# Five block-diagonal blocks, a first block in halves, and search steps spaced by GpSimd's adds, in an FFT convolution with a routed FFN

## The chip, the core and the metric

The kernel runs on one core of a Trainium2 chip. The metric is the device time of one execution in microseconds (us). The core's engines have queues of their own and work side by side: TensorE (PE) multiplies matrices, VectorE (DVE), ScalarE (ACT) and GpSimd (POOL) do the elementwise work, SyncE (SP) issues the transfers. Data lies in SBUF; matmul results go to PSUM, from which another engine must take them.

## The reference

`x` has 8 sequences of 6336 positions and 128 features, `h` one such filter, all in float32. The first part is a causal convolution of every feature by FFT; the second picks the 128 positions with the highest score in each sequence, and adds a gated feed-forward network there and nowhere else.

```python
L = 2 * S                                  # S = 6336
Xf = np.fft.rfft(x, n=L, axis=1)
Hf = np.fft.rfft(h, n=L, axis=0)
y = np.fft.irfft(Xf * Hf[None], n=L, axis=1)[:, :S, :]
...
scores = np.einsum('bsd,d->bs', y, w_gate)
out = y.copy()
for b in range(B):                         # B = 8
    top_idx = np.argpartition(-scores[b], capacity)[:capacity]    # 128
    xe = y[b, top_idx]
    ye = np.maximum(xe @ w1, 0.0) @ w2     # 128 -> 1024 -> 128
    g = 1.0 / (1.0 + np.exp(-scores[b, top_idx]))
    out[b, top_idx] = y[b, top_idx] + g[:, None] * ye
```

## The kernel before

**Tiling.** The transforms are matmuls with tables, with 6336 = 99 x 64. The data is cut into eight units: a pair of sequences (four of them) times a half of the features (two). Unit i has its frequency data in one of two halves of a large SBUF tile (`slots`), i % 2, so that one unit can be transformed while the one before is finished.

**Stages.** Stage A (`stage_a`, L170 to L197) is the transform of 99 points. Its input comes in blocks of 8 per unit: blocks 0 to 7 are the filter `h`, 8 to 15 are unit 0, and 16 + 8i onwards are unit i + 1. `load_x` (L138 to L149) issues a block's load on SP's queue; a paced load has a one-element memset by VectorE ahead of it (L148), which holds it back until VectorE is there. `fold` (L151 to L167) has VectorE make the difference and the sum of a block's two parts. `stage_a` then works in two half blocks (`q` = 0 and 1), each with a PSUM pair of its own: either 16 matmuls of 50 rows and 99 columns (a quartered block, L185), or, for the blocks named in `whole` at L173, 8 matmuls of 128 rows and 198 columns against the block-diagonal table `fa2` (L179). A copy to SBUF follows, by ScalarE (L197) or, where the half is named in `dve`, by VectorE (L194): at the start the second halves of blocks above 9.

Stage B (`stage_b`, L247 to L257) does the second transform in 13 chunks of 8 frequencies (L225), multiplies by the filter (VectorE, L234), and GpSimd adds the two products (L245). `stage_b_first` (L263 to L295) is the joint part, which does the same for the filter and unit 0 together (PE L275, ScalarE L278, VectorE L287, GpSimd L290). Stage C (`stage_c`, from L318) and stage D (`stage_d`, from L354) go back: PE L332 with ScalarE's copy L336, PE L362 with ScalarE's copy L383 and the store to `out`. While stage C runs, VectorE weighs the columns for the scores (L313).

**PSUM.** `psb` hands out three pairs of banks in turn, `psm` two single banks. A tile can be filled again once the one before in its place has been read.

**The route.** For every pair of sequences a generator (`route`) yields between its steps: the scores (L400, L413), a search for the 128th highest key with 6 + 5 digits (`search`, L434 to L463), the places of the chosen rows (L478 to L502), the gather by GpSimd (L525), and then the feed-forward network (`expert`). One search step is a comparison with 7 thresholds (L442), a count (L445), a matmul that sums over the partitions (L451) and three short operations (L454 to L460), all but the matmul on VectorE.

**Order.** Each engine works its queue strictly in order, and the order is written out by a planner with two clocks, `t["pe"]` and `t["dve"]`, which add up constants: 0.7 for a half block of stage A, 0.24 for a frequency of stage B, 0.47 for a column of stage C, 0.89 for a tap of stage D. At a route step's yield, `after_dve(us)` (L56) sets VectorE's clock to the later of both plus `us` plus an allowance, `calm`, and the step after it may be taken 0.3 past that. `aside` (L670s) takes the next step if PE's clock has got there; outside stage D it also asks that VectorE's clock be less than 1.0 past PE's. `aside` is called at most taps of stage D and behind each piece of the plan.

**The main program.** At the start come the loads of the tables and of blocks 0 to 3, 44 small matmuls and a fill of two wide ones (L701) that compute nothing of use, the folds, and 16 blocks of stage A; then the joint part over 13 chunks. Then each unit i runs 32 items, 16 of stage C and 16 of stage D, and a dict `plan` says at which items a half block of unit i + 1 (items 0 to 8) or two of its stage B chunks (items 14 to 28; in unit 6 items 11 to 24) are put between. Unit 7 has nothing to prepare.

Of the kernel before, what the change touches and what calls it, by code (L numbers as in the profile page):

```python
# [12 lines left out]
ALU = mybir.AluOpType  # L13
# [5 lines left out]
N1, N2 = 99, 64  # L19
NE = 50  # L20
NU = 8
# [14 lines left out]
def conv_moe(ctx, tc, x, h, wg_d, w1, w2, fa_d, wb_d, wc_d, at_d, wgl_d, tri_d, cst_d, tw_d, fb_d, *out):  # L36
    nc = tc.nc
    v, act, pool, pe, sp = nc.vector, nc.scalar, nc.gpsimd, nc.tensor, nc.sync
# [7 lines left out]
    t = {"pe": 0.0, "dve": 0.0}  # L46

    def on_pe(us):
        t["pe"] += us

    def on_dve(us):
        t["dve"] = max(t["dve"], t["pe"]) + us

    calm = [0.0]

    def after_dve(us):  # L56
        on_dve(us + calm[0])
        return t["dve"] + 0.3

    due = []  # L60
# [11 lines left out]
    def psb():  # L72
        return pb_.tile([128, 2, 512], F32, tag="b", name="pb")

    def psm():
        return pm_.tile([128, 512], F32, tag="m", name="m")
# [9 lines left out]
    fa = cp.tile([128, 2, N1], F32, name="fa")  # L86
# [17 lines left out]
    acc = cp.tile([128, 2, 2, 2, N1], F32, name="acc")  # L104
# [28 lines left out]
    raw, odd = {}, {}  # L133
    two = cp.tile([128, 2, 512], F32, name="two")

    def load_x(g, paced=False):
        if g >= 8 * (NU + 1):
            return  # L138
        i, n = g // 8 - 1, g % 8
        if i < 0:  # L140
            raw[g] = flat[:, (n + 4) * 1024:(n + 5) * 1024].rearrange("p (s d n) -> p s d n", s=2, d=8)
        elif 8 + RX <= g < 16:
            raw[g] = low(0, 1024, g - 8 - RX).rearrange("p (s d n) -> p s d n", s=2, d=8)
        else:
            raw[g] = tp.tile([128, 2, 8, N2], F32, tag="x", name="xr", bufs=RX)
        src = h if i < 0 else x[i]
        if paced:
            v.memset(raw[g][0:1, 0, 0, 0:1], 0.0)  # L148
        sp.dma_start(out=raw[g].rearrange("p s d n -> p s (d n)"), in_=src[:, n].rearrange("s p w -> p s w"))  # L149

    def fold(g, eng, part=0):  # L151
        if g >= 8 * (NU + 1):
            return
        a = raw[g]
        if g < 16:
            o = low(1, 512, g % 7)
        elif g % 8 % 3 < 2:
            o = two[:, g % 8 % 3]
        else:
            o = low((g // 8 - 1) % 2, 512, 6)  # L160
        odd[g] = o.rearrange("p (d n) -> p d n", d=8)
        o = odd[g]
        if part < 2:
            eng.tensor_tensor(out=o, in0=a[:, 1], in1=a[:, 0], op=ALU.subtract)
        if part != 1:
            eng.tensor_tensor(out=a[:, 0], in0=a[:, 0], in1=a[:, 1], op=ALU.add)  # L166
# [3 lines left out]
    def stage_a(g, r, dve=(), halves=(0, 1)):  # L170
        a, o = raw[g], odd[g]
        n = g % 8
        whole = g in (2, 4, 6, 8, 10, 12)  # L173
        for q in halves:
            pt = psb()
            for d in range(4):
                if whole:
                    for c in range(2):
                        pe.matmul(pt[c * 64:c * 64 + 64, d // 2, d % 2 * 2 * N1:(d % 2 + 1) * 2 * N1],  # L179
                                  (o if c else a[:, 0])[:, q * 4 + d], fa2[:, c], start=True, stop=True)  # L180
                    continue
                for b, c in ((0, 0), (1, 1), (0, 1), (1, 0)):
                    rows = slice(b * 64, b * 64 + NE)
                    src = (o if c else a[:, 0])[rows, q * 4 + d]
                    pe.matmul(pt[c * 64:c * 64 + 64, b, d * N1:(d + 1) * N1], src, fa[rows, c], start=True, stop=True)  # L185
            j = n % 4 * 4 + q * 2
            dst = ys[r].rearrange("p (g b j) k t -> p g b j t k", g=2, b=2)[:, n // 4, :, j:j + 2]
            on_pe(0.7)
            if whole:
                src = pt[:, :, 0:4 * N1].rearrange("p j (t b k) -> p b j t k", t=2, b=2)  # L190
            else:
                src = pt[:, :, 0:4 * N1].rearrange("p b (j t k) -> p b j t k", j=2, t=2)
            if q in dve:
                v.tensor_copy(out=dst, in_=src)  # L194
                on_dve(0.9)
            else:
                act.copy(out=dst, in_=src)  # L197
# [31 lines left out]
    def times(r, ci, banks, ht):  # L229
        k0, kn = kchunks[ci]  # L230
        yv = ys[r].rearrange("p (j c) k t -> p j c k t", c=2)[:, :, :, k0:k0 + kn]

        def mult(dst, c, t):
            v.tensor_tensor(out=dst, in0=banks[c][:, 0:kn * 64].rearrange("p (k b j t) -> p k b j t", k=kn, b=2, t=2),  # L234
                            in1=ht[t].rearrange("p k (j t) -> p k j t", t=2).unsqueeze(2).broadcast_to(
                                [128, kn, 2, 16, 2]), op=ALU.mult)

        for c in range(2):
            tx = tp.tile([128, KC, 64], F32, tag="t", name="tx", bufs=3)[:, 0:kn]
            dst = yv[:, :, c].rearrange("p (b j) k t -> p k b j t", b=2)  # L240
            mult(dst, 0, c)
            mult(tx.rearrange("p k (b j t) -> p k b j t", b=2, t=2), 1, 1 - c)
            on_dve(kn * 0.155)
            d3 = yv[:, :, c].rearrange("p j k t -> p k j t")
            pool.tensor_tensor(out=d3, in0=d3, in1=tx.rearrange("p k (j t) -> p k j t", t=2),  # L245
                               op=ALU.add if c else ALU.subtract)

    def stage_b(i, ci):
        r, u = i % 2, i % 2
        k0, kn = kchunks[ci]  # L250
        pair = psb()
        banks = [pair[:, 0], pair[:, 1]]
        over_k(r, wts.pop((r, ci)), ci, banks)
        ht = hts.pop((u, ci))
        times(r, ci, banks, [ht[:, 0, 0:kn], ht[:, 1, 0:kn]])
        load_w(r, ci + RW)
        later(t["dve"], lambda: load_h(u, ci + RH))  # L257

# [427 lines left out]
    with tc.manual_schedule():  # L686
# [3 lines left out]
        plain = acc.rearrange("p t b c k -> p (t b c k)")[:, 0:128]  # L690
        v.memset(plain, 1.0)
        pt = psb()
# [5 lines left out]
        def fill(n):  # L698
            pt = psm()
            for _ in range(n):  # L700
                pe.matmul(pt, plain, wide, start=True, stop=True)  # L701

        wide = acc.rearrange("p t b c k -> p (t b c k)")[:, 0:512]
        v.memset(wide[:, 128:512], 1.0)
        fill(2)
        pool.memset(fa2, 0.0)
        for o in (0, 1):
# [22 lines left out]
        for i in range(NU):  # L730
# [2 lines left out]
            g0 = 16 + 8 * i  # L733
            plan = {}
            if i < NU - 1:
                for n, at_item in enumerate((0, 0, 0, 2, 2, 2, 4, 4, 4, 6, 6, 6, 8, 8, 8, 8)):
                    plan.setdefault(at_item, []).append(("a", n))
                for n, at_item in enumerate((14, 16, 18, 20, 23, 26, 28) if i < NU - 2 else (11, 13, 16, 18, 20, 22, 24)):
                    plan[at_item] = [("b", k) for k in range(2 * n, min(NC, 2 * n + 2))]
            at_first = 9 if i < NU - 1 else 2  # L740
            calm[0] = 0.45 if i < NU - 1 else 0.0
            for item in range(32):
                place[0] = item
                strand = cs if item < 16 else ds
# [184 lines left out]
```

## Time and profile before

| | us |
|---|---|
| median of 3 runs | 874.43 (874.38 to 876.86) |
| the profiled execution | 875.82 |
| its span, first to last instruction | 874.0 |
| the start, up to the joint part's first full run of matmuls | 41.67 |
| the joint part and the first half blocks of unit 1, up to stage C's first full run | 50.40 (41.67 to 92.07) |
| TensorE's granted clock | 0.999 |

Most of the span's time is in stages C, D, A and B of the eight units. These are the profile's rows for the path that ended last, by line, and for the costliest groups (line, engine, operation, count; busy us, mean ns; idle us just before them and what ended most of it):

```profile
PE 76%; DVE 16%; DMA 3%; issue 3%; POOL 1%; ACT 1%; POOLq 0%; DVEq 0%; ACTq 0%; SPq 0%
...
L332 PE MATMUL pb<-wc,slots 64*99 64x128 f32 x4096 | 236.9, 271 | 1.8 <-POOL slots L290 0.9
L362 PE MATMUL pb<-slots,at 99*99 99x256 f32 (+1 forms) x1056 | 234.0, 374 | 0.6 <-ACT yt L383 0.5
```

A group's idle time counts only on the engine that the row names. The rows of stage C (L332) and stage D (L362) carry 470.9 us of TensorE's work between them and hardly wait.

### The profile page before, as it was taken

The numbers are of one execution on the slowest core, as the hardware profiler recorded it, in microseconds if no ns is written. First come the engines' busy times: TensorE is split into PE (matmuls) and PEld (weight loads), VectorE is DVE, ScalarE is ACT, GpSimd is POOL, SyncE is SP. The second block draws the span as 40 slices with busy tenths as digits, with TensorE's granted clock in tenths as the row PEclk, the third lists the DMA queues.
The fourth block names the chain that finished last, engine by engine and source line by source line (L and its number), as shares of the span: only waits on it lengthen the run. The fifth ranks groups of instructions, "written<-read, shape, count | busy, mean of one in ns | idle before, by whom it ended". The sixth has DMA issues, their size and how long they took to land.

```text
span 874.0 us, 36824 instructions
## 1 busy us (share of the span) xinstructions
PE 852.9 (98%) x16420; PEld 759.4 (87%) x16420; DVE 699.2 (80%) x1609; ACT 348.5 (40%) x407; POOL 323.6 (37%) x269
## 2 busy tenths in 40 slices
PE   9999999999999999999999999999999999999996
PEld 7899898889987998889987899789988899879875
DVE  6678966677599979888399979979379997987771
ACT  5533661157212751157301672137501373125422
POOL 0078106610455016630455105740256304567005
PEclk9999999999999999999999999999999999999999
DMA  8678568766595667666376576845558445752151
GB/s 288 226 251 323 193 194 265 238 191 214 159 286 178 206 189 248 211 196 202 112 227 220 172 226 187 272 152 192 185 152 275 142 156 161 231 164 78 37 184 32
DMA packets 76377, 170.73 MB, mean 195 GB/s; under 512 B 9785, under 2 KB 26135, under 8 KB 76218
## 3 DMA queue, kind: packets, MB, share of 16 engines
q1 hardware_dynamic: 75194, 167.32, 59.6%
q8 instruction: 129, 2.11, 1.0%
q0 software_dynamic: 1024, 1.05, 0.5%
q14 instruction: 30, 0.25, 0.1%
HBM read 135.38 MB, written 32.96 MB: 193 GB/s over the span
## 4 chain that ended last, share of the span: by engine, by line
PE 76%; DVE 16%; DMA 3%; issue 3%; POOL 1%; ACT 1%; POOLq 0%; DVEq 0%; ACTq 0%; SPq 0%
PE pb L332 26%; PE pb L362 18%; PE pb L185 11%; PE pb L225 11%; DVE tx L234 4%; DVE slots L234 4%; PE pb L275 4%; DMA ht<-hd 2%; DVE cmp L442 2%; PE pb L179 2%; PE m L606 1%; PE m L619 1%; PE m L400 1%; DVE num L445 1%; DVE thr L458 1%
## 5 line engine op out<-in xcount | busy, mean ns | idle before, releaser
L245 POOL TENSOR_TENSOR slots<-slots,tx 128x512 f32<-128x512 f32 (+1 forms) x182 | 233.4, 1314 | 427.6 <-DVE tx L234 411.6
L332 PE MATMUL pb<-wc,slots 64*99 64x128 f32 x4096 | 236.9, 271 | 1.8 <-POOL slots L290 0.9
L362 PE MATMUL pb<-slots,at 99*99 99x256 f32 (+1 forms) x1056 | 234.0, 374 | 0.6 <-ACT yt L383 0.5
L332 PEld LDWEIGHTS pb<-wc,slots 64*99 64x99 f32 x4096 | 226.1, 167 | 8.1 <-POOL slots L290 1.3
L362 PEld LDWEIGHTS pb<-slots,at 99*99 99x99 f32 x1056 | 164.3, 163 | 54.3 <-issue 3.9
L383 ACT COPY yt<-pb 99x1024 f32<-99x1024 f32 x63 | 63.9, 1014 | 329.1 <-PE pb L362 316.2
L336 ACT COPY slots<-pb 99x1024 f32<-99x1024 f32 x128 | 143.1, 1118 | 125.1 <-PE pb L332 116.0
L225 PEld LDWEIGHTS pb<-slots 128*64 128x64 f32 x5544 | 168.6, 136 | 16.3 <-issue 14.5
L225 PE MATMUL pb<-slots 128*64 128x64 f32 x5544 | 176.7, 222 | 1.6 <-issue 1.5
L313 DVE SCALAR_TENSOR_TENSOR acc<-slots,wgl,acc 128x198 f32<-128x198 f32 x496 | 170.6, 421 | 0.0
L234 DVE TENSOR_TENSOR slots<-pb,ht 128x512 f32<-128x512 f32 (+1 forms) x182 | 119.7, 658 | 47.1 <-PE pb L225 26.7
L197 ACT COPY slots<-pb 128x792 f32<-128x792 f32 x138 | 115.3, 917 | 16.4 <-PE pb L185 10.7
L234 DVE TENSOR_TENSOR tx<-pb,ht 128x512 f32<-128x512 f32 (+1 forms) x182 | 119.2, 655 | 0.0
L185 PE MATMUL pb<-fa,xr 50*64 50x99 f32 x1856 | 89.7, 248 | 1.4 <-DVE tx L287 0.9
L185 PEld LDWEIGHTS pb<-fa,xr 50*64 50x64 f32 x1856 | 81.2, 133 | 10.4 <-issue 6.1
L185 PE MATMUL pb<-fa,two 50*64 50x99 f32 x1344 | 66.1, 247 | 0.0
L185 PEld LDWEIGHTS pb<-fa,two 50*64 50x64 f32 x1344 | 58.5, 132 | 0.0
L290 POOL TENSOR_TENSOR slots<-slots,tx 128x256 f32<-128x256 f32 (+1 forms) x50 | 39.4, 809 | 51.5 <-DVE tx L287 50.9
L166 DVE TENSOR_TENSOR xr<-xr 128x512 f32<-128x512 f32 x61 | 43.3, 709 | 2.0
L185 PE MATMUL pb<-fa,slots 50*64 50x99 f32 x1024 | 38.3, 248 | 1.7 <-issue 1.7
L445 DVE TENSOR_REDUCE num<-cmp 128x7 bf16<-128x693 bf16 x44 | 38.6, 878 | 1.5
L185 PEld LDWEIGHTS pb<-fa,slots 50*64 50x64 f32 x1024 | 34.5, 134 | 3.6 <-DVE slots L148 1.5
(141 smaller groups left out, 605.0 us busy)
## 6 DMA issues: line engine op xcount, KB each, us to landing
slots<-tab_wb SPq DMA_DIRECT2D x86, 512.0 KB
xr<-in_x SPq DMA_DIRECT2D x61, 512.0 KB
out<-yt SPq DMA_DIRECT2D x63, 396.0 KB
ht<-hd SPq DMA_DIRECT2D x84, 256.0 KB
at<-tab_at SPq DMA_DIRECT2D x128, 153.1 KB
hd<-slots SPq DMA_DIRECT2D x12, 512.0 KB
xr<-tab_wb SPq DMA_DIRECT2D x9, 512.0 KB
slots<-in_h SPq DMA_DIRECT2D x8, 512.0 KB
```

The costliest lines, as they stand in the source:

```text
L166: eng.tensor_tensor(out=a[:, 0], in0=a[:, 0], in1=a[:, 1], op=ALU.add)
L185: pe.matmul(pt[c * 64:c * 64 + 64, b, d * N1:(d + 1) * N1], src, fa[rows, c], start=True, stop=True)
L197: act.copy(out=dst, in_=src)
L225: pe.matmul(banks[c][g * 64:g * 64 + 64, j * 64:j * 64 + 64], wt[:, j, c * 64:c * 64 + 64], y[:, g, :, k0 + j], start=True, stop=True)
L234: v.tensor_tensor(out=dst, in0=banks[c][:, 0:kn * 64].rearrange("p (k b j t) -> p k b j t", k=kn, b=2, t=2), in1=ht[t].rearrange("p k (j t ...
L245: pool.tensor_tensor(out=d3, in0=d3, in1=tx.rearrange("p k (j t) -> p k j t", t=2), op=ALU.add if c else ALU.subtract)
L313: v.scalar_tensor_tensor(out=dst, in0=col, scalar=w, in1=dst, op0=ALU.mult, op1=ALU.add)
L332: pe.matmul(pair[0:N1, g, s % 4 * 128:s % 4 * 128 + 128], y[rows, s // 2, ri, :, s % 2], wc[rows, ri], start=(ri == 0), stop=(ri == 1))
L336: act.copy(out=z[:, s // 4], in_=pair[0:N1].rearrange("p g (j t m) -> p (g j) t m", j=2, t=2))
L362: pe.matmul(pt[0:N1, o:o + w * 128], ats[tau // 2][:, tau % 2, c], z[:, c, q:q + w], start=(c == 0), stop=(c == 1))
L383: act.copy(out=dst, in_=src)
L445: v.tensor_reduce(out=num, in_=cmp, axis=AX.X, op=ALU.add)
```

## The change

It has five parts.

- **The start.** Block 0 is loaded and folded in two halves, and the fill's matmuls have 384 columns instead of 512.
- **Block-diagonal blocks.** `whole` names five blocks, 2, 4, 6, 9 and 12, where it named six, 2, 4, 6, 8, 10 and 12.
- **Copies.** For the last half of block 15 ScalarE copies the first bank and VectorE the second, where VectorE copied both. The first half of block 17 uses two single banks instead of a pair, and ScalarE copies them one by one.
- **The plan of unit 0.** Four half blocks stand at item 0 and three at item 8, where it was three and four. The other units keep their plan.
- **The search's spacing.** Each stage B chunk sets `crowded` to PE's clock plus 1.5. Up to that point `after_dve` adds 1.0, later it adds `calm`, which is 0.2 instead of 0.45 (0 in unit 7, as before). In every unit up to 6 the step that follows is thus placed by whether a chunk, and so GpSimd's adds, is near.

```diff
-    calm = [0.0]
+    calm, crowded = [0.0], [0.0]
...
-        on_dve(us + calm[0])
+        on_dve(us + (calm[0] if t["pe"] > crowded[0] else 1.0))
...
         src = h if i < 0 else x[i]
+        if g == 0:
+            for q in range(2):
+                sp.dma_start(out=raw[g][:, :, q * 4:q * 4 + 4].rearrange("p s d n -> p s (d n)"),
+                             in_=src[:, n, :, q * 256:q * 256 + 256].rearrange("s p w -> p s w"))
+            return
...
         o = odd[g]
+        if g == 0:
+            for q in range(2):
+                d = slice(q * 4, q * 4 + 4)
+                eng.tensor_tensor(out=o[:, d], in0=a[:, 1, d], in1=a[:, 0, d], op=ALU.subtract)
+                eng.tensor_tensor(out=a[:, 0, d], in0=a[:, 0, d], in1=a[:, 1, d], op=ALU.add)
+            return
...
-        whole = g in (2, 4, 6, 8, 10, 12)
+        whole = g in (2, 4, 6, 9, 12)
         for q in halves:
-            pt = psb()
+            if g == 17 and q == 0:
+                pt = [psm(), psm()]
+            else:
+                pair = psb()
+                pt = [pair[:, 0], pair[:, 1]]
...
             on_pe(0.7)
+            if g == 17 and q == 0 or g == 15 and q == 1:
+                for b in range(2):
+                    src = pt[b][:, 0:4 * N1].rearrange("p (j t k) -> p j t k", j=2, t=2)
+                    if b and g == 15:
+                        v.tensor_copy(out=dst[:, b], in_=src)
+                    else:
+                        act.copy(out=dst[:, b], in_=src)
+                continue
...
         times(r, ci, banks, [ht[:, 0, 0:kn], ht[:, 1, 0:kn]])
+        crowded[0] = t["pe"] + 1.5
...
-                pe.matmul(pt, plain, wide, start=True, stop=True)
+                pe.matmul(pt[:, 0:384], plain, wide, start=True, stop=True)
...
-                for n, at_item in enumerate((0, 0, 0, 2, 2, 2, 4, 4, 4, 6, 6, 6, 8, 8, 8, 8)):
-                    plan.setdefault(at_item, []).append(("a", n))
+                for n in range(16):
+                    plan.setdefault(min(2 * ((n if i else max(n - 1, 0)) // 3), 8), []).append(("a", n))
...
-            calm[0] = 0.45 if i < NU - 1 else 0.0
+            calm[0] = 0.2 if i < NU - 1 else 0.0
```

More of the change, by code (lines that the diff above doesn't have):

```diff
@@ L178, in stage_a @@
                     for c in range(2):
-                        pe.matmul(pt[c * 64:c * 64 + 64, d // 2, d % 2 * 2 * N1:(d % 2 + 1) * 2 * N1],
+                        pe.matmul(pt[d // 2][c * 64:c * 64 + 64, d % 2 * 2 * N1:(d % 2 + 1) * 2 * N1],
                                   (o if c else a[:, 0])[:, q * 4 + d], fa2[:, c], start=True, stop=True)
@@ L184, in stage_a @@
                     src = (o if c else a[:, 0])[rows, q * 4 + d]
-                    pe.matmul(pt[c * 64:c * 64 + 64, b, d * N1:(d + 1) * N1], src, fa[rows, c], start=True, stop=True)
+                    pe.matmul(pt[b][c * 64:c * 64 + 64, d * N1:(d + 1) * N1], src, fa[rows, c], start=True, stop=True)
             j = n % 4 * 4 + q * 2
@@ L188, in stage_a @@
             on_pe(0.7)
+            if g == 17 and q == 0 or g == 15 and q == 1:
[6 more added lines that the diff above has]
+                continue
             if whole:
-                src = pt[:, :, 0:4 * N1].rearrange("p j (t b k) -> p b j t k", t=2, b=2)
+                src = pair[:, :, 0:4 * N1].rearrange("p j (t b k) -> p b j t k", t=2, b=2)
             else:
-                src = pt[:, :, 0:4 * N1].rearrange("p b (j t k) -> p b j t k", j=2, t=2)
+                src = pair[:, :, 0:4 * N1].rearrange("p b (j t k) -> p b j t k", j=2, t=2)
             if q in dve:
@@ L700, in fill @@
             for _ in range(n):
-                pe.matmul(pt, plain, wide, start=True, stop=True)
-        wide = acc.rearrange("p t b c k -> p (t b c k)")[:, 0:512]
-        v.memset(wide[:, 128:512], 1.0)
+                pe.matmul(pt[:, 0:384], plain, wide, start=True, stop=True)
+        wide = acc.rearrange("p t b c k -> p (t b c k)")[:, 0:384]
+        v.memset(wide[:, 128:384], 1.0)
         fill(2)
```

## The prediction

> **What bounds the kernel now.** I read the page first, for the shares of the engines.
>
> ```profile
> PE 852.9 (98%) x16420; PEld 759.4 (87%) x16420; DVE 699.2 (80%) x1609; ACT 348.5 (40%) x407; POOL 323.6 (37%) x269
> ```
>
> TensorE (PE) is busy 98% of the span, so only two kinds of edit can help: fewer matmul microseconds, or work put where PE stands idle. The second view, the waits of PE alone (who was waited for: total, times, longest), says where it stands.
>
> ```profile
> PE m L451 <- DVE num L445: 3.4, 6, 0.8
> ...
> PE pb L332 <- POOL slots L290: 0.9, 2, 0.6
> PE pb L185 <- DVE tx L287: 0.9, 1, 0.9
> PE pb L275 <- DVE slots L194: 0.8, 1, 0.8
> ```
>
> The largest item is the search step: its matmul (L451) waits for VectorE's count (L445). L332 behind GpSimd and L185 behind L287 are the seam between the joint part and the first unit; L275 behind L194 is the start of the joint part. All four are short: what can be won is a few microseconds. The third view is busy time by stretch (stretch, us, PE, PEld, DVE, ACT, POOL, PEclk, DMA share, GB/s), for stage D of unit 1 and for the end of unit 6.
>
> ```profile
> 233.00:283.00 50.00, 49.20 (x774) 40.23 (x769) 48.53 (x94) 7.11 (x7) 28.30 (x22) 1.00 0.73 232
> 740.00:788.00 48.00, 47.67 (x713) 39.37 (x713) 43.00 (x97) 9.25 (x9) 30.68 (x23) 1.00 0.63 199
> ```
>
> In 233 to 283 VectorE is busy 48.5 of 50 us. There a wait taken off PE can come back as a late VectorE product. That caution decides how much of the search edit I count.
>
> **The start: block 0 in halves, a shorter fill.**
>
> ```profile
> 3.57 3.78 PE L701 MATMUL m<-acc 128*128 128x512 f32 x4
> 7.28 1.97 PE L185 MATMUL pb<-fa,slots 50*64 50x99 f32 x64
> ```
>
> ```profile
> 6.39 0.69 DVE L166 TENSOR_TENSOR slots<-slots 128x512 f32<-128x512 f32 x1
> ...
> 7.74 0.69 DVE L166 TENSOR_TENSOR slots<-slots 128x512 f32<-128x512 f32 x1
> ```
>
> Block 0's fold ends at 6.39 + 0.69 = 7.08 and its matmuls start 0.20 later, at 7.28. With half the data and half the fold the first matmuls could start about 1.1 us earlier; the fill, 384 columns for 512, ends about 0.9 earlier (3.78 x 1/4) and is out of the way. But block 1 follows, and its fold ends at 7.74 + 0.69 = 8.43 whatever block 0 does, so block 1 cannot start before 8.63. Today it starts when block 0 is done, near 7.28 + 1.53 = 8.81. So of 1.1 us **0.2** can be kept. The halves cost one more DMA issue ahead of block 1's and twice the packets for block 0; VectorE does four half folds for two (estimate +0.2 us, before block 1's data is there). Bounds: 0.4 gained if the earlier reissue on the SP queue (block 4's load follows block 0's fold) helps the DMA stream, 0.3 lost if block 1 lands later.
>
> [...] Matmuls of L185 in two equal stretches (x in the PE column):
>
> ```profile
> 7.30:7.90 0.60, 0.60 (x16) 0.60 (x20) 1.00 1.04 396
> 8.30:8.90 0.60, 0.60 (x39) 0.60 (x32) 1.00 1.01 283
> ```
>
> Of the same shape, 16 touch the first 0.6 us and 39 the second, though the clock column says 1.00 in both: PE runs at under half its pace until about 8.1. [...]
>
> **Six block-diagonal blocks become five: 2, 4, 6, 9, 12.**
>
> ```profile
> 27.00 1.52 PE pb L185 x62
> ...
> 32.88 2.83 PE pb L179 x32
> ```
>
> A quartered block takes 1.52 us of PE, a block-diagonal one 2.83, so one fewer removes 1.31. But this is not all kept. VectorE's queue is in order, and block 10's second half is copied out by VectorE (blocks above 9), behind the fold of block 15:
>
> ```profile
> 30.79 0.69 DVE L166 TENSOR_TENSOR slots<-slots 128x512 f32<-128x512 f32 x1
> 31.43 0.98 DVE L194 COPY slots<-pb 128x792 f32<-128x792 f32 x1
> ```
>
> The fold of block 15 ends at 31.48, the copy at 32.41. With blocks 8 and 10 quartered blocks 8 to 11 take 1.52 + 2.83 + 1.52 + 1.52 = 7.39 from block 8's start (27.00 - 2.83 = 24.17), and PE is done with block 11 at 31.56. But there are three PSUM pairs, and block 12's first half needs the pair that this copy frees, 32.41 + 0.1. It starts today at 32.88 (chain). So **0.3** is kept of 1.31, for about 1.0 goes into a new wait for L194 which no row of before shows. Bounds: nothing, if block 15's data lands as late and the copy later; 1.31, if the fold comes earlier.
>
> **Block 15's last half copied by two engines.**
>
> ```profile
> 40.54 1.00 DVE slots L194
> 41.53 0.14 issue
> 41.67 4.34 PE pb L275 x72
> ```
>
> ```profile
> 39.85 0.89 ACT L197 COPY slots<-pb 128x792 f32<-128x792 f32 x1 [1.00 <-PE pb L185]
> ```
>
> The joint part starts 0.14 after VectorE's copy. ScalarE is free at 39.85 + 0.89 = 40.74; half a copy is some 0.5, so both halves are there at 41.25: **0.3** gained. Bounds 0.1 (ScalarE's half as long as a whole) and 0.45.
>
> **Four half blocks behind the joint part.** Half a quartered block is 1.52 / 2 = 0.76. It moves from item 8 of unit 0, where the chain has PE alone, to item 0, where PE waits twice:
>
> ```profile
> 113.25 2.93 PE pb L185 x124
> ```
>
> ```profile
> 91.04 0.47 PE L332 MATMUL pb<-wc,slots 64*99 64x128 f32 x4 [0.34 <-POOL slots L290]
> 92.07 3.53 PE L332 MATMUL pb<-wc,slots 64*99 64x128 f32 x60 [0.56 <-POOL slots L290]
> ```
>
> PE idles 0.34 before 91.04, so the three halves of before end at 90.70; the fourth ends near 91.46, and stage C still cannot go on before GpSimd's last add lets it, at 92.07. The first part of block 17 goes to the small PSUM tiles, so that no pair is missing for the fourth half; its two ScalarE copies beside one cost nothing, as ScalarE's next work comes from the 92.07 row. **0.7** gained; bounds 0.3 (the four matmuls of 91.04 move behind 92.07, and a pair may come free only with the joint part's last read) and 0.76. What is late next is the same GpSimd add.
>
> **The search steps.** Each step issues one matmul and seven VectorE operations. Its place in PE's order comes from the planner: at issue its VectorE clock is raised by 2.35 plus an allowance, and the next step is taken at the first slot at which the PE clock is 0.3 past it. Before, the allowance is 0.45 everywhere. After, it is 1.0 where a stage B chunk lies within 1.5 us, else 0.2. I followed both clocks by hand from the constants (0.7 a half block, 0.24 a frequency of stage B, 0.89 a tap of stage D). For units 1, 3 and 5: the first step stands right behind a chunk at PE clock 174.06. Old: 178.00 + 2.80 + 0.3 = 181.10, and the slot behind the next two chunks is 181.46. New: 178.52 + 3.35 + 0.3 = 182.17, so it misses 181.46 and takes 182.35, one tap later. The third step keeps its slot, the fourth falls behind one chunk more, the fifth moves 3.56 later, the sixth 0.89. For units 2 and 4 every search step keeps its slot (the largest sum, 275.81, is just under its slot 275.87). What these slots cost today:
>
> ```profile
> 251.88 0.17 PE L451 MATMUL m<-num,block 128*128 128x7 bf16 x1 [0.57 <-DVE num L445]
> ```
>
> ```profile
> 349.27 0.17 PE L451 MATMUL m<-num,block 128*128 128x7 bf16 x1 [0.78 <-DVE num L445]
> ```
>
> The first is the second step of unit 1, and one tap (0.89) is more than 0.57: the wait goes, in units 1, 3 and 5. The second is a step of unit 2: this wait, and unit 4's, stay. With the small wait of the fourth step I count 0.7 each, 2.1 in all, less what VectorE gives back: its order of work hardly changes, so it is no faster. At the end of unit 1 the fold for the next block must be ready:
>
> ```profile
> 281.53 0.69 DVE L166 TENSOR_TENSOR xr<-xr 128x512 f32<-128x512 f32 x1
> ```
>
> ```profile
> 283.04 2.21 PE pb L185 x92
> ```
>
> It ends at 282.22 and PE uses it at 283.04. A PE that comes 0.7 earlier comes at 282.3, just behind it. I take 0.2 off each: **1.5**. Bounds: nothing (the late fifth and sixth steps push that fold 0.7 back) and 2.1.
>
> Why a step is slow at all:
>
> ```profile
> 248.92 2.00 DVE L442 TENSOR_TENSOR cmp<-hf,thr 128x693 bf16<-128x693 f32 x1
> ...
> 258.53 0.87 DVE L442 TENSOR_TENSOR cmp<-hf,thr 128x693 bf16<-128x693 f32 x1
> ```
>
> ```profile
> L245 POOL TENSOR_TENSOR slots<-slots,tx 128x512 f32<-128x512 f32 (+1 forms) x182 | 233.4, 1314 | 427.6 <-DVE tx L234 411.6
> ```
>
> The same compare takes 0.87 or 2.00; the difference, 1.13, is near one GpSimd add, 1.31 in the mean. [...]
>
> In unit 6 the sum comes out otherwise: at item 11 the VectorE clock stands 1.15 past PE's (637.49 against 636.34) where a step may be taken below 1.0 (before: 636.85). So the first step of the second search is not taken there but at item 16, and every later step one slot on.
>
> ```profile
> 740.28 2.00 PE L332 MATMUL pb<-wc,slots 64*99 64x128 f32 x32 [0.39 <-DVE tx L234]
> ```
>
> VectorE's products of the four chunks at items 11 and 13 stand behind that step's operations, and PE waits 0.39 for the last of them. Without the step the wait goes: +0.4. In return VectorE has a step more behind 742, up to 3.4 us, where it is busy 43 of 48; I take 0.3 off for PSUM pairs that come free later there. **0.1**, bounds -1 and +0.5.
>
> **Sum**: 0.2 + 0.3 + 0.3 + 0.7 + 1.5 + 0.1 = 3.1 us off the profiled execution's span of 874.0. That execution took 875.82, the median of the runs is 874.43: the difference lies around the span and is not touched, so the forecast is 874.4 - 3.1 = **871.3**.
>
> **The rivals.** (1) VectorE is the bound in stage D and gives the search gain back at each unit's first fold: 0.2 + 0.3 + 0.3 + 0.7 = 1.5, so 872.9. For it: 48.5 busy of 50. Against it: PE meets that fold with 0.8 us to spare today. (2) All is kept: the whole 1.31, 0.45, 0.76, 2.1, 0.5 and 0.3 at the start, 5.4, so 869.0. Against it: the copy behind block 15's fold. (3) PE idles for a microsecond between block 0 and block 1's fold, and the full pace comes only after block 1: its 1.52 us at 16 for 39 take 2.2 us more, so 873.5. For it: the two counts. Against it: most of the fill and all of block 0 still stand ahead of 8.1. [...] (4) Slower: the end of unit 6. VectorE weighs all 64 columns before the scores can start:
>
> ```profile
> 780.72 21.56 DVE L313 SCALAR_TENSOR_TENSOR acc<-slots,wgl,acc 128x198 f32<-128x198 f32 x64
> ```
>
> ```profile
> 805.51 0.35 PE L400 MATMUL m<-wc,acc 128*99 128x128 f32 x1
> ```
>
> ```profile
> 783.61 19.48 POOL L525 DMA_INDIRECT xe<-out,iu  x1 [0.30 <-issue]
> ```
>
> The slack is 805.51 - 802.28 = 3.2 us. The later search puts its remaining steps between these weighings and moves two gathers into the last unit, where one of today's four is held 19.48 us until the weighing ends. Past 3.2 us each further one is a us on PE and on the end. I count 2.4 of delay; at 6.9 (every moved operation contended) the wait is 3.7 and the time 871.3 + 3.7 = 875.0. To lose more than 0.3% it must be 9.
>
> **How the numbers follow.** About 0.3% (2.6 us) is what a measurement of this kernel can tell from no change: under 871.8 is faster, over 877.0 slower. Chances: forecast 0.52, rival 1 0.25, rival 2 0.12, rival 3 0.06, rival 4 0.05. The forecast's own spread is about 1 us, from 870.3 to 872.4: of its 0.52 some 0.38 lies under 871.8, of rival 1 some 0.03, and all of rival 2, 0.53 faster together; 0.02 is slower, rival 4's far end; the rest, 0.45, is the same. The range from 868.8 to 873.8 takes in rivals 1 to 3 and leaves out rival 4 and the tails.
>
> **What would show it.** The L451 waits of units 1, 3 and 5 gone, two of about 0.8 left in units 2 and 4; a new wait of about 1 us of block 12's matmuls for L194; the joint part's first full run near 40.9 and stage C's, 92.07 before, near 91.2; item 8 of unit 0 with three halves (2.2 us) for four (2.93); the first search matmul at item 11 of unit 6 gone. Wrong would be: the same L451 total, a wait of L185 for a fold at 282 to 283, L400 waiting for L313, or a start at the slow pace past 8.1.

## The result: slower by 0.55%, and the profile after

The changed kernel took 880.04 us (median of 22 runs) where the kernel before took 875.03 (22 runs). The ratio is 1.0055, with a 95% interval of 1.0037 to 1.0072: about 4.8 us slower, where 3.1 us faster was forecast and the range ended at 873.8. The profiled execution has a span of 879.2 us for 874.0.

In these two executions the loss stands in the first 100 us, and the rest of the changed kernel is 0.9 us faster. These are first matmuls, from the traces of the two profiled executions (us from the span's start):

| | before | after | later by |
|---|---|---|---|
| block 0 | 7.28 | 9.50 | 2.2 |
| block 2 | 10.54 | 14.61 | 4.1 |
| joint part, first full run | 41.67 | 47.74 | 6.1 |
| stage C of unit 0, first full run | 92.07 | 98.17 | 6.1 |
| end of the span | 874.0 | 879.2 | 5.2 |

The chain that ended last, of the changed kernel, at the start (start us, us, what). Line numbers are those of the changed kernel: stage A is L194 (block-diagonal) and L200 (quartered), VectorE's copy L217, the joint part L299.

```profile
1.22 3.21 DMA slots<-in_h
4.43 0.02 issue
4.45 4.01 DMA slots<-in_h
...
9.50 5.18 PE pb L200 x127
...
28.59 6.53 DMA slots<-in_x
...
36.63 0.91 DVE slots L217
37.54 0.04 issue
37.58 4.58 PE pb L194 x32
...
47.74 12.28 PE pb L299 x200
```

The two half loads of block 0 stand one behind the other. In the kernel before the chain of the start holds no transfer at all:

```profile
1.06 2.57 PE pb L695 x88
3.64 3.71 PE m L701 x4
7.35 3.27 PE pb L185 x121
```

The waits of SP's queue in the changed kernel, first 40 us (who was waited for: total, times, longest), name what holds them up:

```profile
SPq L149 <- DMA slots<-in_h: 2.8, 1, 2.8
```

L149 is the load of a half. SP waits 2.8 us for the first half to land before it issues the second, and everything behind it in SP's queue, the loads of blocks 1 to 15, comes later too. Then blocks 0 and 1 take 5.18 us on TensorE for the 3.27 that the same 128 matmuls took before (a few are missing from each count): it had stood idle for 3.0 us before 9.50 and runs them at a slow pace (24 matmuls touch the 0.6 us from 10.50 and again those from 13.50, where 39 touched the 0.6 us from 8.30 before; the clock column says 1.00 in all three). At the end of stage A the data of block 15 is late again, the copies behind its fold are late with it, and block 12 takes 4.58 us for 2.83. A wait of 1.4 us, named "issue", ends at 36.49 in front of it; what such waits are is found below. Here the clock column shows the slow pace (stretch, us, PE, PEld, DVE, ACT, POOL with counts, PEclk, DMA share, GB/s):

```profile
35.00:40.00 5.00, 2.87 (x24) 2.04 (x23) 3.17 (x4) 0.33 (x1) 0.00 (x0) 0.80 0.74 247
40.00:50.00 10.00, 9.06 (x252) 7.97 (x250) 3.53 (x4) 4.13 (x6) 0.00 (x0) 0.93 0.20 57
```

This second slow stretch doesn't belong to every execution: in another profile of the same kernel (e9 below) block 12 takes 2.90 us and the joint part starts at 44.33.

Behind 90 us the waits of TensorE have changed as well. The changed kernel, 90 to 860 us (L356 is stage C, L386 stage D, L475 the search's matmul):

```profile
PE pb L200 <- issue: 3.6, 4, 1.6
PE m L475 <- DVE num L469: 1.4, 2, 0.8
PE pb L356 <- issue: 1.1, 2, 0.7
PE pb L386 <- DVE ge L478: 1.1, 1, 1.1
```

The search step's wait (L475, which was L451) is down from 3.4 us to 1.4, as meant. But the waits that end with "issue", for nothing that the profile shows, have grown. The same view of the kernel before, same window:

```profile
PE pb L185 <- issue: 1.9, 3, 1.1
PE pb L225 <- issue: 1.5, 4, 0.4
...
PE pb L332 <- issue: 0.5, 1, 0.5
```

3.9 us there, 5.1 here (with 0.4 of L248). As a sum that is no more than chance: a second profile of the kernel before has 5.3 (e5 below). It was the places of these waits that led on.

### The profile page after: what moved, and what is told of

It reads as the page before. It is cut to its first block, busy times and chain, and to the rows that moved or that the text cites. A ratio compares the mean times of both kernels' runs of the same rounds, so it can differ in the third digit from the quotient of the medians.

```text
span 879.2 us, 36898 instructions
## 1 busy us (share of the span) xinstructions
PE 853.5 (97%) x16452; PEld 760.8 (87%) x16452; DVE 698.6 (79%) x1611; ACT 349.7 (40%) x409; POOL 316.7 (36%) x269
## 3 DMA queue, kind: packets, MB, share of 16 engines
q8 instruction: 129, 2.11, 1.0%
## 4 chain that ended last, share of the span: by engine, by line
PE 76%; DVE 17%; issue 3%; DMA 3%; ACT 1%; POOL 1%; POOLq 0%; SPq 0%; DVEq 0%; ACTq 0%
PE pb L356 26%; PE pb L386 19%; PE pb L248 11%; PE pb L200 11%; DVE tx L257 5%; DVE slots L257 4%; PE pb L299 4%; DVE cmp L466 3%; PE pb L194 1%; PE m L630 1%; PE m L643 1%; DVE thr L482 1%; PE m L424 1%; DMA slots<-in_h 1%; DMA slots<-in_x 1%
## 5 line engine op out<-in xcount | busy, mean ns | idle before, releaser
L356 PE MATMUL pb<-wc,slots 64*99 64x128 f32 x4096 | 237.7, 271 | 1.7 <-issue 1.1
L386 PE MATMUL pb<-slots,at 99*99 99x256 f32 (+1 forms) x1056 | 235.0, 375 | 1.6 <-DVE ge L478 1.1
L356 PEld LDWEIGHTS pb<-wc,slots 64*99 64x99 f32 x4096 | 226.7, 167 | 8.4 <-issue 1.8
L386 PEld LDWEIGHTS pb<-slots,at 99*99 99x99 f32 x1056 | 163.9, 163 | 53.7 <-issue 1.6
L248 PEld LDWEIGHTS pb<-slots 128*64 128x64 f32 x5544 | 168.0, 136 | 14.6 <-issue 13.0
L248 PE MATMUL pb<-slots 128*64 128x64 f32 x5544 | 175.1, 222 | 0.6 <-issue 0.4
L257 DVE TENSOR_TENSOR slots<-pb,ht 128x512 f32<-128x512 f32 (+1 forms) x182 | 119.7, 658 | 48.9 <-PE pb L248 23.9
L257 DVE TENSOR_TENSOR tx<-pb,ht 128x512 f32<-128x512 f32 (+1 forms) x182 | 119.2, 655 | 0.0
L200 PE MATMUL pb<-fa,xr 50*64 50x99 f32 x1872 | 90.8, 247 | 3.5 <-issue 2.0
L200 PEld LDWEIGHTS pb<-fa,xr 50*64 50x64 f32 x1872 | 82.3, 133 | 10.5 <-issue 5.5
L200 PE MATMUL pb<-fa,two 50*64 50x99 f32 x1328 | 65.9, 247 | 1.6 <-issue 1.6
L200 PEld LDWEIGHTS pb<-fa,two 50*64 50x64 f32 x1328 | 58.0, 132 | 1.8 <-issue 1.8
L200 PE MATMUL pb<-fa,slots 50*64 50x99 f32 x1056 | 40.8, 258 | 4.4 <-DVE slots L172 3.0
L200 PEld LDWEIGHTS pb<-fa,slots 50*64 50x64 f32 x1056 | 37.5, 142 | 7.1 <-DVE slots L172 4.2
```

Of the source, the lines that this page charges most:

```text
L200: pe.matmul(pt[b][c * 64:c * 64 + 64, d * N1:(d + 1) * N1], src, fa[rows, c], start=True, stop=True)
L248: pe.matmul(banks[c][g * 64:g * 64 + 64, j * 64:j * 64 + 64], wt[:, j, c * 64:c * 64 + 64], y[:, g, :, k0 + j], start=True, stop=True)
L356: pe.matmul(pair[0:N1, g, s % 4 * 128:s % 4 * 128 + 128], y[rows, s // 2, ri, :, s % 2], wc[rows, ri], start=(ri == 0), stop=(ri == 1))
L386: pe.matmul(pt[0:N1, o:o + w * 128], ats[tau // 2][:, tau % 2, c], z[:, c, q:q + w], start=(c == 0), stop=(c == 1))
```

## The experiments

All kernels were timed in turn with runs of the kernel before on the same chip, and the ratios are to those. From one chip to another the time of the kernel before moves by some tenths of a per cent (medians of 878.04 to 878.95 us in the experiments, 875.03 in the first measurement), so the ratios compare, not the microseconds.

### The start by itself, and everything but the start

My theory was that the second half's load had cost it all. Four kernels: the changed kernel with the old start; with block 0 in one load; with the halves stored so that they do not touch; and the kernel before with the new start alone.

**e1_start_old**: one load and one fold for block 0, fill 512 wide.

```diff
-        if g == 0:
-            for q in range(2):
-                sp.dma_start(out=raw[g][:, :, q * 4:q * 4 + 4]...
...
-                pe.matmul(pt[:, 0:384], plain, wide, start=True, stop=True)
+                pe.matmul(pt, plain, wide, start=True, stop=True)
```

> The changed kernel with the whole start as it was: block 0 in one load and one fold, the fill 512 wide. All other parts stay changed. Theory A (the start costs it all, since the second half's load waits until the first half has landed: 3.21 us of one load, then 4.01 of the other in the chain): the joint part's first full run comes back from 47.74 to about 41.4, TensorE does not wait before its first block, and the time is 873.5 to 875. Theory B (the other parts, among them the copies behind block 15's fold, lose it): block 12 still waits about 2 us and the time stays near 879.

**e2_load_whole**: only the half loads are taken out.

> The changed kernel with block 0 loaded by one transfer, its fold still in halves and the fill still 384 wide. Theory A: no wait of the second load, so block 0's first matmul is at about 6.6 us (9.50 in the changed kernel, 7.28 before), the joint part's first full run near 41.2, time 873 to 875, the same as with the old start or 0.2 less. Rival C (the shorter fill lets TensorE fall back to the slow pace): first two blocks take 5 us instead of 3.3, the time is 1.5 to 2 us above that with the old start.

**e3_halves_apart**: the halves lie one behind the other in memory.

```diff
-                sp.dma_start(out=raw[g][:, :, q * 4:q * 4 + 4].rearrange("p s d n -> p s (d n)"),
+                sp.dma_start(out=flat[:, (n + 4) * 1024 + q * 512:(n + 4) * 1024 + q * 512 + 512].rearrange(
+                                 "p (s w) -> p s w", s=2),
                              in_=src[:, n, :, q * 256:q * 256 + 256].rearrange("s p w -> p s w"))
```

> The changed kernel with block 0's two halves stored one behind the other, so that the two loads write ranges that do not overlap; the transfers are the same in number, size and run length, and neither waits. Theory A: first half there before 5.5, first matmul at 5.9 to 6.6, joint part near 41, time 873 to 875. Rival D (two loads of 1 KB runs are slow by themselves): block 0's first matmul stays near 9 us and the time near 879.

**e4_only_start**: the kernel before, with the half loads, the half folds and the fill of 384.

> The kernel before with the start alone changed (two half loads, half folds, the shorter fill). Theory A: as in the changed kernel the second load waits, first matmul near 9.5 and slow to about 14.6; later blocks catch up a little; joint part 3.5 to 6 us later than 41.67, time 878.5 to 881, slower than before by 0.4 to 0.7%. Theory B: within 0.5 us of before.

| | ratio | 95% | first matmul | joint part |
|---|---|---|---|---|
| e1, old start | 1.0046 | 1.0025 to 1.0067 | 7.28 | 41.66 |
| e2, one load | 1.0048 | 1.0024 to 1.0072 | 6.44 | 41.34 |
| e3, halves apart | 1.0047 | 1.0020 to 1.0075 | 6.43 | 44.31 |
| e4, only the start | 1.0047 | 1.0025 to 1.0069 | 9.68 | 45.38 |

The start is what I took it for. e4's chain has the same two loads:

```profile
1.21 3.46 DMA slots<-in_h
...
4.68 3.96 DMA slots<-in_h
...
9.68 5.49 PE pb L196 x128
```

Both e2 and e3, which have no such wait, bring the first matmul to 6.4. SP's second half load waits 2.8 us for the first in the changed kernel and 3.0 in e4; in e3 SP's queue has no such wait. The halves are strided (each takes 256 of every 512 elements, for both parts), so the range from the first to the last element of one overlaps that of the other, and a wait was put in for a clash that does not exist: e3 changes where the halves lie and nothing of the transfers, and the wait is gone. VectorE's first half fold waited for both halves too (8.56 in the changed kernel, 4.51 in e3). And even without the wait the halves bring nothing: in e3 the first half is folded from 4.51 (5.49 in e2), but block 1's fold begins at 8.15 where e2's begins at 7.10, and TensorE stands idle from 8.56 to 9.67. (e3's late joint part, 44.31, has another reason: a wait of 2.4 us named "issue" that ends at 33.84, of the kind below, with the clock at 0.50 behind it.)

But the theory that the start cost it all fell. With the old start (e1) the joint part was back at 41.66, and the time was still 0.46% over; e2, at 41.34, was no better. The start costs 0.47% (e4), and something of the rest costs as much again.

### Where TensorE's instructions lie

What e1 to e3 had in common with each other and not with the kernel before was seen in their waits named "issue". In e1 to e3, behind 90 us, they came to 9.1, 6.0 and 7.9 us; in e4, which has the start alone, to 4.6. They also stood at other places. The trace's record of transfers has a queue for instructions (q8: 129 packets, 2.11 MB, so 16.4 KB each). Set beside the waits of the changed kernel, the last packet of that queue ahead of each:

```
TensorE resumes   packet starts   takes   between
302.66            300.30          0.93    2.36
602.85            600.51          0.94    2.34
704.34            701.98          0.93    2.36
710.95            708.50          0.98    2.45
```

Each of these waits ends 2.3 to 2.5 us after such a packet starts. Over all seventeen profiles, from 90 to 860 us, 100 of the 101 waits named issue in stages A and C end 2.1 to 2.8 us after one; the packets come some 6.7 us apart in the mean, so this isn't chance. I read it so: TensorE has run out of instructions and waits for the next piece. (Of the short ones in stage B, L225 in the kernel before, only 3 of 71 fit this, and what they wait for stays open.) The bytes agree with it: 2.11 MB for 16420 matmuls and 16420 weight loads, the counts of the kernel before, are 64 bytes for each of 32840 instructions, and a packet holds some 255 of them (an estimate, which takes the whole queue for TensorE's). In stage A's quartered blocks a piece lasts only 3.0 us (128 instructions in 1.52). The wait at 710.95 and the transfers around it (queue: packets, MB, share of the 16 engines from 708 to 711):

```profile
710.95 0.30 PE L200 MATMUL pb<-fa,two 50*64 50x99 f32 x2 [1.57 <-issue]
```

```profile
q1 hardware_dynamic: 439, 1.14, 100.4%
q8 instruction: 1, 0.02, 2.0%
```

The piece was asked for while the data queue (q1) took 100.4% of the 16 engines.

Now the set of five block-diagonal blocks gives one block 32 matmuls instead of 16. Each stands in the profile as two matmuls with a weight load each (x32 for the 16 of block 12), and the changed kernel has 16452 of both where the kernel before has 16420, so the block has 64 more instructions: 4 KB, a quarter of a piece. Everything behind block 12 lies 4 KB further on. That is theory G, and it can be tested without touching anything else, by the number of small warm-up matmuls at the start.

**e5_before_again**, a control: the kernel before, unchanged.

> The kernel before, unchanged, timed against itself: a control. It must come out at 0.998 to 1.002 of the kernel before if the comparison is fair. Its profile also says how much the waits named issue move from one execution to the next: 6 to 9 us in all behind 90 us if they are drawn anew each time, at the same places as in the first profile (near 192, 298, 437, 641, 712).

**e6_five_grid_back**: e1, with fewer warm-up matmuls.

```diff
-        for k in range(44):
+        for k in range(27):
...
-                pe.matmul(pt, plain, wide, start=True, stop=True)
+                pe.matmul(pt[:, 0:384], plain, wide, start=True, stop=True)
...
-        fill(2)
+        fill(3)
```

> The changed kernel with the old start, but 27 small warm-up matmuls for 44 and three fills 384 wide for two of 512: 16 matmuls fewer, as many as the five-block set adds, so that behind block 12 TensorE's instructions lie on the same 16 KB pieces as in the kernel before. Theory G (the change moved the pieces in which TensorE's instructions are fetched against the dense matmuls of stage A, and the late ones cost 4 us): waits named issue return to 192, 298, 437, 641 and 712, 6 to 7 us in all behind 90 us, and the time is 0.3% under to 0.1% over the kernel before. Rival S (the search spacing and the plan lose it in stages D): the time stays 0.4 to 0.5% over.

**e7_before_grid**: the kernel before, with 60 for 44 and a fill 384 wide.

> The kernel before with 60 warm-up matmuls for 44 and the fill 384 wide: the same length of warm-up to 0.1 us, but TensorE's instructions lie 4 KB later, as in the changed kernel. Nothing else differs. Theory G: waits named issue near 111, 294, 313, 517 and 603 as in the changed kernel with the old start, 8 to 11 us in all, time 0.3 to 0.5% over the kernel before. Rival S: 0.999 to 1.001.

**e8_six_blocks**: e1, with `whole = g in (2, 4, 6, 8, 10, 12)`.

> The changed kernel with the old start and the old six block-diagonal blocks; spacing, plan and copies stay changed. TensorE's pieces lie as before. Theory G: no wait of 1.4 us before block 12, joint part at 41.4, time 0.1 to 0.3% under the kernel before. Rival S: 0.3 to 0.5% over.

| | ratio | 95% | "issue" behind 90 us |
|---|---|---|---|
| e5, control | 1.0006 | 0.9979 to 1.0032 | 5.3 |
| e6, five blocks, pieces back | 0.9998 | 0.9976 to 1.0020 | 3.6 |
| e7, before, pieces 4 KB on | 1.0059 | 1.0033 to 1.0085 | 6.8 |
| e8, six blocks | 0.9984 | 0.9960 to 1.0009 | 3.4 |

Theory G held in both directions. e7 differs from the kernel before only in its warm-up, and loses 0.59%. e6 has the whole of the change but the start, and loses nothing. Rival S fell. What missed is the size of the waits: each of the three sums for which a figure was expected (e5, e6, e7) came out lower, and e7's 6.8 us are only some 2.5 above the mean of the profiles with the pieces as before, while e7 lost about 5.2. A wait is counted from the modelled end of the last matmul, so the sums understate the loss: in e11 (below) one of 0.33 us, ending at 98.61, goes with 0.71 us more than e8 takes from stage C's first full run to its second. How the rest of the 5.2 comes about isn't shown. The rows of e7 and then of e6 (L185 and L189 are stage A, L225 and L237 stage B, L332 and L345 stage C):

```profile
PE pb L185 <- issue: 4.2, 6, 1.0
...
PE pb L225 <- issue: 2.0, 5, 0.4
...
PE pb L332 <- issue: 0.6, 2, 0.3
```

```profile
PE pb L237 <- issue: 1.6, 4, 0.4
...
PE pb L189 <- issue: 1.1, 2, 0.7
...
PE pb L345 <- issue: 0.9, 1, 0.9
```

### Do the two add, and are there better places?

**e9_after_again** is the changed kernel once more, on the chip of e10 to e12, six runs of it. **e10_after_grid_back** is the changed kernel with 28 warm-up matmuls for 44. **e11_best** leaves out the half loads and the five-block set. **e12_before_grid2** is the kernel before with 76 warm-up matmuls and a fill 256 wide.

> The changed kernel unchanged, on the chip of the runs before it. If the late second load (alone 1.0047 of the kernel before) and the moved instruction pieces (alone 1.0059) add, it comes out at 1.008 to 1.011, less the 0.2% that plan, copies and spacing bring. If it is again near 1.0055, the two overlap: a kernel whose transfers run 4 to 6 us later does not meet the same late fetches.

> The changed kernel with 28 small warm-up matmuls for 44 and nothing else: TensorE waits for the late first block in any case, so the shorter warm-up costs nothing there, and behind block 12 its instruction pieces lie as in the kernel before. If the two causes add: 0.3 to 0.5% faster than the changed kernel, 1.002 to 1.005 of the kernel before. If they overlap: the same as the changed kernel within 0.15%.

> The changed kernel with block 0 loaded by one transfer (its fold still in halves, the fill 384 wide) and with the six block-diagonal blocks of before, which also put the instruction pieces back. What is left of the change: half folds, shorter fill, copies, plan of unit 0, spacing. Both theories: first matmul at 6.5, no 1.4 us wait before block 12, waits named issue behind 90 us 3.4 to 5.3 us; 0.15 to 0.35% faster than the kernel before.

> The kernel before with 76 warm-up matmuls for 44 and a fill 256 wide: the same length of warm-up to 0.1 us, TensorE's instructions 8 KB later, half a piece. Theory G gives no sign for this place, only that the time can move by some tenths of a per cent with the sum of the waits named issue behind 90 us: 4.2 us on average where the pieces lie as before, 7.0 where they lie 4 KB later. If the place of the pieces did not matter, and it were the number of warm-up matmuls that cost 0.59%, this kernel would lose twice as much, 1.01 or more.

| | ratio | 95% | "issue" behind 90 us |
|---|---|---|---|
| e9, changed kernel again | 1.0079 | 1.0064 to 1.0094 | 6.1 |
| e10, its pieces put back | 1.0034 | 1.0012 to 1.0057 | 3.7 |
| e11, without both | 0.9992 | 0.9973 to 1.0011 | 4.8 |
| e12, before, pieces 8 KB on | 1.0028 | 1.0011 to 1.0044 | 6.4 |

On this chip the two add. The start alone cost 0.47% (e4) and the pieces 0.59% (e7) or 0.45% (e9 less e10); less the 0 to 0.2% that the rest brings (e6, e8, e11), that is close to the changed kernel's 0.79%. The first measurement of the same kernel gave 0.55%; the two intervals just meet, and the ratio of 22 runs is the one to quote. By that ratio the two would add only in part, so that each of them costs is shown, and that they add in full is not. e11, for which 0.15 to 0.35% faster than the kernel before was expected, shows no gain. And e12 speaks against the warm-up matmuls themselves: 32 more cost 0.28%, not twice the 0.59% of 16 more.

### The rest of the change

**e13_unit6_old** is e8 with unit 6's steps put back (allowance 0.45 and no `crowded` there, and `t["dve"] < t["pe"] + 1.2` in `aside`). **e14_only_spacing** is the kernel before with `crowded` and 0.2 and nothing else. **e15_before_grid3** is the kernel before with 27 warm-up matmuls and three fills of 384, which puts the pieces 4 KB the other way.

> As the run with the old start and six blocks (0.9984 of the kernel before), but in unit 6 the search steps stand as in the kernel before: the old allowance there, and a step may be taken up to 1.2 us of lead where it was 1.0. If the later steps of unit 6 give the spacing's gain back: stage D of unit 6 at 41.7 us for 43.1, no wait of 1.1 us for the ge operation, time 0.1 to 0.2% under that run, 0.996 to 0.998 of the kernel before. If not: 0.998 to 1.000.

> The kernel before with the search spacing alone. As predicted (1.5 + 0.1 us): 0.998. As the stage times of the other runs say: stage D of units 3 and 5 0.5 us shorter each, of unit 1 between 0.4 shorter and 0.4 longer, of units 2 and 4 the same, of unit 6 1.35 longer; 0.9995 to 1.0005.

> The kernel before with 27 small warm-up matmuls for 44 and three fills 384 wide for two of 512: TensorE's instructions lie 4 KB earlier, the fourth place of four. If before's place is a lucky one: 1.002 to 1.006. If the moved place is the unlucky one (the other two at 1.000 and 1.0028): 0.999 to 1.002.

e13 came out at 0.9984 (0.9966 to 1.0001), e14 at 0.9978 (0.9957 to 0.9998), e15 at 1.0019 (0.9990 to 1.0048, unclear). Stage D by unit, from its first matmul to the next unit's first of stage C, in us:

| unit | 1 | 2 | 3 | 4 | 5 | 6 |
|---|---|---|---|---|---|---|
| before | 49.06 | 49.36 | 49.13 | 49.29 | 49.07 | 41.70 |
| e5, before | 49.91 | 49.26 | 49.07 | 49.35 | 49.05 | 41.69 |
| e14, spacing alone | 48.53 | 49.26 | 48.50 | 49.28 | 48.58 | 43.09 |
| e13, unit 6 as before | 48.65 | 49.26 | 48.63 | 49.37 | 48.55 | 41.77 |

The spacing does what it says in units 1, 3 and 5, and nothing in 2 and 4. In unit 6 it costs 1.4. VectorE's queue in the changed kernel shows why (start us, us, operation):

```profile
771.80 2.00 DVE L466 TENSOR_TENSOR cmp<-r,thr 128x693 bf16<-128x693 f32 x1
773.83 0.88 DVE L469 TENSOR_REDUCE num<-cmp 128x7 bf16<-128x693 bf16 x1
774.62 0.68 DVE L257 TENSOR_TENSOR slots<-pb,ht 128x512 f32<-128x512 f32 x1
...
778.80 0.69 DVE L257 TENSOR_TENSOR tx<-pb,ht 128x512 f32<-128x512 f32 x1
779.40 0.16 DVE L478 TENSOR_SCALAR_CACHE_REDUCE ge<-m 128x7 f32<-128x7 f32 x1
```

The step that now comes one slot later puts its comparison and count ahead of the products of two chunks (L257). These empty the PSUM pairs, and stage D's next matmul starts at 779.63, once the last product is done (779.49). The profile puts its wait of 1.1 us down to the `ge` operation right behind that product; that the pair is what it waits for is my reading of the order. e13 takes that wait away, but its ratio is that of e8, 0.9984 both, so a gain of 1.3 us from it is not shown in the time. e14, the spacing alone, is the one kernel whose interval lies below 1, by a hair and as one of fifteen: a gain is likely, not shown.

## Why the prediction was wrong, point by point

**The start, 0.2 won: wrong, and the step that failed is a sentence.** I wrote that the halves "cost one more DMA issue ahead of block 1's and twice the packets for block 0". They cost a wait of the second issue for the landing of the first, 2.4 to 3.0 us on SP's queue. The bounds, 0.3 lost at worst, didn't hold it: in four profiles with that wait the joint part began at 47.74, 45.38, 44.33 and 44.62, where it began at 41.5 to 42.8 with the old start (before, e1, e5, e6, e8, e13, e14, e15; later in e7 and e12, where a wait for a piece stands ahead of it), and the time says 0.47% (e4). The pace of TensorE had a part, as in rival 3, but behind an idle time that I hadn't foreseen: blocks 0 and 1 took 5.2 to 5.5 us for 3.3. The shorter fill as such cost nothing that shows (e2's first full run of the joint part comes at 41.34, before e1's). One figure of the sum was off as well: I had block 1 start at 8.81, with block 0 at full pace, where the trace of the kernel before has it at 9.07.

**Five blocks for six, 0.3 kept of 1.31: the mechanism was right, the sum left out a cost.** The wait behind block 15's fold is there. In e6, with the pieces back, the chain goes from VectorE's copy (L206 in e6) to block 12 (L183), through the quartered blocks (L189) and the copies of block 15 (ScalarE L209 and L199, VectorE L197), and on to the joint part (L288):

```profile
31.29 0.69 DVE slots L166
31.98 0.91 DVE slots L206
32.88 0.04 issue
32.93 2.90 PE pb L183 x32
35.83 3.90 PE pb L189 x151
39.75 0.73 ACT slots L209
40.52 0.53 ACT slots L199
41.07 0.58 DVE slots L197
41.65 0.04 issue
41.70 18.34 PE pb L288 x306
```

Block 12 starts at 32.93 where it started at 32.88, so all of the 1.31 is eaten, not 1.0 of it. What I left out altogether is that fewer microseconds of matmuls came with 64 more instructions, and that these move the pieces in which all later instructions come. I had seen waits named issue in the profile before and took them as fixed. This term, which I had put at nothing, costs more than any that I counted: 0.59% (e7) is 5.2 us.

**Block 15's last half by two engines, 0.3 won: wrong.** The three rows ahead of the last two show it: ScalarE's half (40.52) and VectorE's (41.07) run one after the other. VectorE waited 1.0 us for ScalarE. Why isn't shown: unlike block 0's halves, these write ranges of `slots` that don't overlap, by the kernel's own indices. From the last stage A matmul's end to the joint part's first full run it took 1.19 us before and takes 1.31 after: 0.1 lost.

**Four half blocks at item 0, 0.7 won: right.** From the joint part's first full run to unit 1's first matmul of stage C it took 144.20 before and 144.12 in e5; in the changed kernel, e6, e8 and e9 it takes 143.49 to 143.60. That is 0.5 to 0.7. In all of these no wait named issue falls into that stretch, and the clock column says 1.00 throughout. With such a wait it takes 144.1 to 145.0 with the new plan and 145.0 to 145.5 with the old. Item 8 came out as forecast too, 2.21 us in e8 for 2.93.

**The search steps, 1.5 + 0.1 won: units 1, 3 and 5 right, unit 6 wrong.** Every step stands where I put it: the waits of the second steps of units 1, 3 and 5 are gone, those of units 2 and 4 stayed (L475 waits twice, 0.8 at most), and unit 6's first step of the second search is gone from item 11. Stage D gained 0.5 to 0.6 in units 3 and 5 of e14; unit 1's is less sure (48.5 in e14, 49.4 in e8, 49.1 and 49.9 in the kernel before). Unit 6's term, 0.1 won with bounds from -1 to +0.5, is off: 1.4 lost in its stage D, outside the bounds. By these stage times e14 wins 0.4 us against the first profile of the kernel before and 1.1 against the second, not 1.6. Its ratio says 0.22%, 1.9 us, with an interval from 0.2 to 3.8 that takes in all of these; if the sum is right, that is luck. That a compare is slow beside a GpSimd add, both traces show: in the kernel before 16 of the 44 compares overlap adds (L245) for 1.25 us or more and take 2.00 us (13 of them) or 1.27, and the other 28 overlap them by 0.07 at most and take 0.87 to 0.89. In the changed kernel 10 of the 44 take 2.00, each beside an add, and none 1.27.

**The rivals.** None of the four came. The slower one, which I gave 0.05, needed a wait for the weighing at the end of unit 6; there is none. Its 6.9 us, with every moved operation contended, are shown by no run; what the changed kernel shows is the last weighing ending at 809.38, 2.0 us before the scores' first matmul (811.37). Both causes of the loss lie in what I didn't ask of each edit: what its transfer has to wait for, and how many instructions it issues on TensorE.

## What to carry to other kernels

Before splitting a transfer into halves, look at the range from first to last element of each half: the strided halves of block 0 overlap as ranges, and the second got a wait of 2.8 us for the first, in SP's queue where all later loads stand behind it. Where an engine is busy 98% of the time with short instructions, count an edit's instructions as well as its microseconds, and try the same kernel with its instructions some KB further on before believing a few tenths of a per cent: here 4 KB of warm-up alone moved the time by 0.59%, more than any gain that the edits brought.

## What the runs showed of the hardware

**The place of the instructions.** Nine profiles with the pieces as before have 3.4 to 5.3 us of waits named issue behind 90 us, 4.3 in the mean; six with the pieces 4 KB on have 5.1 to 9.1, 6.8 in the mean. The four places give 1, 1.0059, 1.0028 and 1.0019 (unclear): none was seen better than the one that the kernel before has. Why one place is worse, when in each unit the pieces fall on stage A's dense runs in several ways, wasn't settled; that a piece starts late while the data queues are full is read from the records and wasn't tried by itself.

**Behind three waits of 1.8 to 2.1 us TensorE's clock fell to 0.50 to 0.53.** In e1 a wait named issue of 2.1 us ends at 293.59. The clock behind it:

```profile
292.00:294.00 2.00, 0.41 (x7) 0.41 (x8) 2.00 (x7) 0.20 (x1) 0.00 (x0) 0.98 0.85 250
294.00:296.00 2.00, 2.00 (x23) 2.00 (x21) 1.97 (x5) 0.00 (x0) 0.00 (x0) 0.50 0.69 259
296.00:298.00 2.00, 2.00 (x29) 2.00 (x28) 2.00 (x7) 1.09 (x1) 0.00 (x0) 0.66 0.00 0
```

In e12 it fell behind a wait of 1.8 us, which ends at 315.49:

```profile
316.00:318.00 2.00, 2.00 (x36) 1.88 (x30) 2.00 (x8) 0.89 (x1) 0.00 (x0) 0.75 0.12 34
318.00:320.00 2.00, 2.00 (x22) 2.00 (x22) 2.00 (x7) 0.52 (x1) 0.00 (x0) 0.50 0.86 293
```

And so it did behind one of 2.0 us that ends at 716.59 in e4 (0.53 from 718 to 720). But the length alone doesn't decide. Waits of 1.5 and 1.6 us (e11, and 710.95 in the changed kernel) left the clock at 1.00, and so did one of 2.0 us in e1 itself, which ends at 718.45, and one of 2.3 us ahead of block 12 in e6:

```profile
718.00:720.00 2.00, 1.55 (x57) 1.42 (x59) 1.97 (x6) 0.75 (x1) 0.00 (x0) 1.00 0.03 9
```

So a late piece costs its wait and sometimes some 1.7 us more (an estimate from e1's rows: 2 us at 0.50 and 2 at 0.66). What else decides isn't shown.
